# Spectral mixing, then a leaky-ReLU MLP: the exchange of real and imaginary products in the second batch, by DMA for every group instead of every other one

## The chip, the cores and the metric

The kernel runs on one core of a Trainium2 chip. The core has a matrix engine (TensorE, "PE" in the profile, with "PEld" for the loading of weights), a vector engine (VectorE, "DVE"), a scalar engine (ScalarE, "ACT"), GpSimd ("POOL") and SyncE ("SP"), which here only issues DMAs. The metric is the device time of one execution in microseconds, lower is better.

## What is computed

The reference, cut to what matters:

```python
X = np.fft.rfft(x, axis=1)                     # x: 8 x 3008 x 256, fp32
Y = X * (filt_r + 1j * filt_i)[None, :, :]
y = np.fft.irfft(Y, n=3008, axis=1)
h = y.reshape(24064, 256) @ w_in               # 256 x 2048
g = np.maximum(0.01 * h, h)
out = g @ w_out                                # 2048 x 256
```

## The kernel before

The Fourier transforms are matrix products: 3008 is 94 x 32, so each transform is a product with a 94-point matrix, a change of layout, and a product with 32-point matrices that also hold the twiddle factors. All matrix operands are fp16, sums are fp32 in PSUM.

The eight batches b = 0 to 7 follow each other. Each batch goes through four stages, each cut into groups:

- `s1_group` (lines 249 to 261, 16 groups): one matmul on the rows of x (L254), a copy to SBUF, and a store to the DRAM buffer `dz1` (L259). `t1_load` (L266) reads it back in the new layout, as `z1`.
- `s2_group` (lines 297 to 319, 12 groups): two matmuls (L303) give 128 x 512 fp32 in a PSUM bank. Partitions 0 to 63 hold real parts, 64 to 127 imaginary parts. The complex product with the filter needs `ps * fa` (p1, L315) plus the same bank times `fb` with the two halves of partitions exchanged (p3). GpSimd adds the two as `y` (L318).
- `sa_group` (12 groups): one matmul on `y` (L325), a copy by ACT (L327), a store to `dz2` (L329). `t2_load` (L273) reads it back as `z2`.
- `sb_group` (16 groups): four matmuls (L346) and a copy give `yt`, the input of the MLP.

The exchange of halves in `s2_group` is made in two ways. As a rule VectorE writes `p2 = ps * fb` (L312), and two DMAs on SP's queue copy its halves crosswise into p3 (L313, L314). In the second batch (b = 1), where g is even (`EXG = 0`), VectorE writes p3 itself with two products on 64 partitions each (L309, L310), which read one half of the bank and write the other half of p3.

p1, p2 and p3 are tiles of 128 x 512 fp32 from the pool `scr`, which has three buffers for each of the three tags. Six more tiles with the same tags (`spare`) serve the first batch, two of each tag.

The first batch (b = 0) is written out step by step in a table and takes about 34 us. After that the MLP runs in chunks of 512 tokens: `moe1` makes h (L505) with ACT applying the leaky ReLU (L510), and `plain` (L630, the first chunks) or `products` (L569, a fast scheme with seven products) make the output. The groups of the transforms of later batches are put between the MLP's matmuls.

The order of all this is a plan worked out at build time: each piece of work gets a time in units of an eighth of a chunk, and `work`, a heap, hands the pieces out in order of time. `at` and `soon` put pieces on it; `soon(AFTER[1], ...)` puts the two exchange DMAs 0.8 units after the product, and `y_delay` says how long after the group the add on GpSimd stands: 1.2 units where VectorE exchanges, 3.17 (`AFTER[3]`) for the other groups of b = 1, 1.33 (`AFTER[2]`) for later batches. Once made, the order on each engine is fixed; each engine, and each queue of DMAs (SP's, GpSimd's), works through its own list in order and waits where a tile is not ready. GpSimd's list also has the loads of x for the next batch (L191).

The small groups (L254, L303, L325, L346, and the last groups of the first batch, L437) take turns on two PSUM banks, called `pf` in the profile like a third one that holds the output of the MLP. Finished outputs are copied to SBUF by VectorE (L635 in the first chunks) and stored by SP (L556).

Of the kernel before, what the change touches and what calls it, by code (L numbers as in the profile page):

```python
# [11 lines left out]
P = 128  # L12
FP16 = mybir.dt.float16
FP32 = mybir.dt.float32
AL = mybir.AluOpType
# [60 lines left out]
def kernel(  # L76
# [9 lines left out]
    nc = tc.nc  # L86
    B, N, D = x.shape
# [8 lines left out]
    SL = 8  # L96
    NCH = NCT // 2
    QT = 4 * N1
    W0 = 3
    GAP = 0.6  # L100
    EXG = 0
    LANDED = 2.43
    READ = 2.2
    SUMS = (0.09, 1.59, 2.35, 4)
# [5 lines left out]
    AFTER = (0.53, 0.8, 1.33, 3.17, 0.39, 0.52)  # L110
# [31 lines left out]
    scrp = ctx.enter_context(tc.tile_pool(name="scr", bufs=3))  # L142
# [11 lines left out]
    def bank(kind, n, w):  # L154
        of = wide if kind == "ph" else single
        t = of[turn[kind] % len(of)]
        turn[kind] += 1
        return t[:, : n * w].rearrange("p (n w) -> p n w", n=n)
# [5 lines left out]
    def at(time, f):  # L164
        clock["n"] += 1
        heapq.heappush(work, (time, clock["n"], f))
# [4 lines left out]
    def need(*what):  # L171
        for w in what:
            assert w in issued, w

    def noted(what, f):
        f()
        issued.add(what)

    def soon(delay, f):
        at(clock["now"] + delay, f)  # L180
# [5 lines left out]
    DH = D // 2  # L186
# [105 lines left out]
    ys = {}  # L292

    def y_delay(b, g):
        return 1.2 if b == 1 and g % 2 == EXG else AFTER[2] if b > 1 else AFTER[3]

    def s2_group(b, g):
        def go():
            ps = bank("pf", 2, D)
            need(("z1", b, g // 2), ("f2t",))  # L300
            issued.add(("s2", b, g))
            for j in range(2):
                nc.tensor.matmul(ps[:, j, :], f2_sb[:, 2 * g + j, :],  # L303
                                 z1[g // 2 % 4][:, 2 * (g % 2) + j, :],
                                 start=True, stop=True)
            fa, fb = fa_sb[:, ds(2 * g, 2), :], fb_sb[:, ds(2 * g, 2), :]
            p1, p2, p3 = (scrp.tile([P, 2, D], FP32, tag=f"p{i}", name=f"p{i}_b{b}_g{g}") for i in (1, 2, 3))
            if b == 1 and g % 2 == EXG:
                nc.vector.tensor_tensor(p3[0:64], ps[64:P], fb[64:P], AL.mult)  # L309
                nc.vector.tensor_tensor(p3[64:P], ps[0:64], fb[0:64], AL.mult)  # L310
            else:
                nc.vector.tensor_tensor(p2[:], ps, fb, AL.mult)  # L312
                soon(AFTER[1], lambda: nc.sync.dma_start(p3[0:64], p2[64:P]))  # L313
                soon(AFTER[1], lambda: nc.sync.dma_start(p3[64:P], p2[0:64]))  # L314
            nc.vector.tensor_tensor(p1[:], ps, fa, AL.mult)  # L315
            ys[(b, g)] = y1 = ypp.tile([P, 2, D], FP16, tag="y", name=f"y_b{b}_g{g}")
            soon(y_delay(b, g), lambda: noted(
                ("y", b, g), lambda: nc.gpsimd.tensor_tensor(y1[:], p1[:], p3[:], AL.add)))  # L318
        return go
# [13 lines left out]
    def quad_copy(h, dt, ps, copy):  # L333

        yv = yt[:, dt, ts(h, QT)].rearrange("p (a c) -> p a c", c=4)
        copy(yv, ps.rearrange("p c a -> p a c"))  # L336

    def sb_group(b, g, copy):
        h, dt = g // 2, g % 2

        def go():
            ps = bank("pf", 4, N1)
            need(("z2", b, h), ("i1t",))
            issued.add(("sb", b, g))
            for j in range(4):
                nc.tensor.matmul(ps[:, j, :], z2[h % 4][:K4, j, ts(dt, P)], i1_sb[:K4, 4 * h + j, :],  # L346
                                 start=True, stop=True)
            quad_copy(h, dt, ps, copy)
        return go
# [6 lines left out]
    prods = [gtp.tile([P, 2, NC, DH], FP16, tag="gt", padded_shape=[P, 2, Q, DH], name=f"prod{hf}")  # L356
             for hf in range(2)]
    first_banks = single + wide
    held, spare = {}, [scrp.tile([P, 4, DH], FP32, tag=f"p{i // 2 + 1}", name=f"spare{i}") for i in range(6)]
    engine = {"A": act, "D": dve}  # L360

    def fill(key, b, n, w):
# [185 lines left out]
    def store(ci, tj, of, queue=nc.sync):  # L548
# [3 lines left out]
        while t < end:  # L552
            e = min(end, (t // QT + 1) * QT)
            b, h = divmod(t // QT, N2 // 4)
            row = b * N + (t % QT) // 4 * N2 + 4 * h
            queue.dma_start(  # L556
# [35 lines left out]
    def last_product(ci):  # L592
        def after(po):
            add(rows(ci, 0)[:, :, 1], po, rows(ci, 1)[:, :, 2], AL.add)
            soon(AFTER[5], lambda: stores(ci, 0))
        return product(ci, lambda: sum_places(ci)[3], b22, after, 3)

    def products(ci):
        a11, a12, a21, a22 = (lambda i=i, j=j: quarter(ci, i, j) for i in range(2) for j in range(2))

        def after5(po):
            add(rows(ci, 1)[:, :, 1:3], twice(po), part[1], AL.add)
            soon(AFTER[5], lambda: stores(ci, 1))

        def m1():
            return product(ci, a11, b11, lambda po: nc.scalar.copy(t1, po))

        def m2():
            return product(ci, a12, b21, lambda po: add(rows(ci, 0)[:, :, 0], po, t1, AL.add))

        def m7():
            return product(ci, lambda: sum_places(ci)[1], wt[2], lambda po: add(v7, po, t1, AL.add), 1)

        if ci == NCHUNK - 1:
            items = last_product(ci - 1) + m1() + m7() + m2()
        elif ci > W0:
            items = m1() + last_product(ci - 1) + m2() + m7()
        else:
            done["products"] += 1
            items = m1() + [lambda: None] * (2 * NCH) + m2() + m7()  # L620
        items += product(ci, lambda: sum_places(ci)[2], wt[1], lambda po: add(part[1], twice(po), part[0], AL.add), 2)
        items += product(ci, a22, wt[3], lambda po: add(rows(ci, 1)[:, :, 0], po, u3, AL.add))
        items += product(ci, lambda: sum_places(ci)[0], wt[0], after5, 0)
        return items + last_product(ci) if ci == NCHUNK - 1 else items

    def plain(ci):

        def one(tj, ct):
            po = out_banks[(done["products"] + tj) % 2].rearrange("p a t d -> p (a t d)")[:, :D]
            nc.tensor.matmul(po, gts[ci][:, ct, ts(tj, P)], w_out_sb[:, ct, :],  # L630
                             start=(ct == 0), stop=(ct == NCT - 1))
            if ct < NCT - 1:
                return
            ot = outp.tile([P, D], FP32, tag="ost", padded_shape=[P, 6 * P], name=f"ost_c{ci}_t{tj}")
            nc.vector.tensor_copy(ot[:], po)  # L635
            soon(AFTER[5], lambda: store(ci, tj, ot[:]))
        return [lambda tj=tj, ct=ct: one(tj, ct) for tj in range(4) for ct in range(NCT)]
# [5 lines left out]
    def plan(b, s1, s1_step, s2, s2_step, lag, sb, sb_step, xl, x_step):  # L643
# [9 lines left out]
        for g in range(16):  # L653
            due = SL * (QT * (8 * b + g // 2) // CH)
            groups.append((min(sb + sb_step * g, due - DUE[0] + DUE[1] * (g % 2)), 4, b, g, sb_group(b, g, act)))
# [13 lines left out]
    for b in range(1, B):  # L669
        z = 47 * (b - 4) if b > 4 else 0  # L670
        p = PLANS[min(b, 4) - 1]
# [18 lines left out]
    while queue:  # L690
        time, n, stage, b, g, f = heapq.heappop(queue)
        t = max(time, last + GAP)
        if stage == 3:
            behind = when[2, b, g] + y_delay(b, g) + 0.02 if (2, b, g) in when else None
        else:
            behind = load_time(stage - 1, b, g // 2) if stage != 1 else 0
            if stage != 1 and behind is not None:
                behind += READ
        if behind is None or behind + 0.02 > t:
            heapq.heappush(queue, (t + GAP if behind is None else behind + 0.03, n, stage, b, g, f))  # L700
            continue
        when[stage, b, g] = last = t
        at(t, f)
        if stage in (2, 4) and g % 2:
            place[stage - 1, g // 2 % 4] = t + 0.1
        assert stage < 4 or t < SL * (QT * (8 * b + g // 2) // CH), (b, g, t)

    for ci in range(NCHUNK + 1):
# [3 lines left out]
        if ci == 0:  # L712
            continue
        wino = W0 <= ci - 1
        items = products(ci - 1) if wino else plain(ci - 1)
# [38 lines left out]
```

## Time and profile before

| | |
|---|---|
| median of 3 runs | 749.61 us (749.38 to 750.32) |
| the profiled execution | 749.61 us |
| its span, first to last instruction | 747.8 us |
| granted TensorE clock | 0.999 |
| DMA traffic | 113.64 MB, mean 152 GB/s |
| first batch, before the MLP starts | about 34 us |
| second batch's `s2` groups | 59.9 to 91.5 us |
| second batch's `sa` groups | 70.1 to 100.8 us |
| third batch's `s2` groups begin | 118.3 us |

The profile is of one execution. A page sums it up: busy time of each engine, the chain of work that ended last, the costliest groups of instructions. Views of its trace show the engines by stretches of time, what each engine waited for, and the instructions in order of time. In a timeline a line has the start in us, the length in us, the engine ("SPq" is the issue of a DMA by SP), the line of the kernel, the operation, what it writes and reads, and in brackets how long the engine was idle before it and what ended that.

### The profile page before, as it was taken

The page shows a single profiled execution, that of the slowest core. Times are in us where ns is not written, and L with a number is a line of the kernel's source. Part 1 is how long each engine was busy: PE and PEld are TensorE (multiplying, and loading weights), DVE is VectorE, ACT ScalarE, POOL GpSimd, SP SyncE. Part 2 cuts the span into 40 slices and gives each one's busy share as a digit, 9 for nine tenths or more (in the row PEclk, how much of TensorE's full clock was granted, in tenths as well). Part 3 has the DMA queues.
Part 4 walks back from the last instruction along what each step waited for, and adds up shares of the span by engine and source line. Part 5 has one row for each costly group of instructions (what it writes and reads, how often), then busy time and mean ns, then how long its engine had stood idle before and what let it go on. Part 6 is the DMA issues. An engine that isn't in the chain of part 4 may idle for free.

```text
span 747.8 us, 19408 instructions
## 1 busy us (share of the span) xinstructions
PE 737.9 (99%) x8017; PEld 528.6 (71%) x8017; DVE 499.9 (67%) x684; ACT 559.1 (75%) x755; POOL 167.5 (22%) x171
## 2 busy tenths in 40 slices
PE   8999999999999999999999999999999999999996
PEld 3556667776787777877778777777777777777775
DVE  6977647766686666776767667766676675565565
ACT  4776797888878787877777778787777777777662
POOL 6503422332323213221222322121212220000000
PEclk9999999999999999999999999999999999999999
DMA  9997798887876666755675656544454333111111
GB/s 207 228 222 190 187 226 222 210 193 202 208 189 149 161 183 175 169 142 161 195 173 150 158 165 170 157 131 111 143 168 119 97 108 104 50 56 53 34 52 59
DMA packets 119560, 113.64 MB, mean 152 GB/s; under 512 B 16352, under 2 KB 92768, under 8 KB 119280
## 3 DMA queue, kind: packets, MB, share of 16 engines
q1 hardware_dynamic: 104127, 94.66, 43.0%
q0 software_dynamic: 15056, 17.49, 15.9%
q8 instruction: 62, 1.02, 0.6%
q10 hardware_dynamic: 289, 0.26, 0.1%
q14 instruction: 26, 0.21, 0.1%
HBM read 57.51 MB, written 50.33 MB: 144 GB/s over the span
## 4 chain that ended last, share of the span: by engine, by line
PE 93%; DMA 2%; DVE 2%; ACT 1%; issue 0%; POOL 0%; SPq 0%; DVEq 0%; POOLq 0%
PE ph L505 42%; PE po_ps L569 18%; PE pf L569 18%; PE pf L254 3%; PE pf L346 3%; PE pf L303 2%; PE pf L325 2%; DMA p_b_g<-p_b_g 2%; PE pf L630 1%; PE po_ps L630 1%; DMA big<-in_x_dram 1%; PE po_ps L368 1%; POOL y_b_g L318 0%; ACT yt L336 0%; PE ph L396 0%
## 5 line engine op out<-in xcount | busy, mean ns | idle before, releaser
L510 ACT ACTIVATE gt_c<-ph 128x1024 f16<-128x1024 f32 x376 | 385.3, 1025 | 135.2 <-PE ph L505 123.5
L505 PE MATMUL ph<-yt,w_in_sb 128*128 128x512 f16 (+7 forms) x1728 | 447.5, 351 | 0.2 <-ACT yt L336 0.2
L569 PEld LDWEIGHTS <-gt_c 128*128 128x128 f16 x2800 | 202.1, 98 | 91.3 <-issue 0.2
L318 POOL TENSOR_TENSOR y_b_g<-p_b_g,p_b_g 128x512 f16<-128x512 f32 x84 | 117.8, 1403 | 415.0 <-DMA p_b_g<-p_b_g 255.2
L569 PEld LDWEIGHTS <-big 128*128 128x128 f16 x2128 | 151.2, 98 | 61.6 <-issue 0.2
L505 PEld LDWEIGHTS <-w_in_sb 128*128 128x128 f16 x1728 | 137.4, 98 | 20.3 <-issue 0.7
L312 DVE TENSOR_TENSOR p_b_g<-pf,fb_sb 128x512 f32<-128x512 f32 x78 | 53.7, 688 | 32.3 <-PE pf L303 17.2
L569 PE MATMUL po_ps<-wt_sb,gt_c 128*128 128x128 f16 x704 | 70.0, 219 | 0.0
L569 PE MATMUL pf<-wt_sb,gt_c 128*128 128x128 f16 x688 | 68.5, 219 | 0.0
L569 PE MATMUL pf<-w_out_sb,gt_c 128*128 128x128 f16 x720 | 68.0, 219 | 0.0
L569 PE MATMUL po_ps<-wt_sb,big 128*128 128x128 f16 x720 | 67.5, 219 | 0.0
L569 PE MATMUL pf<-wt_sb,big 128*128 128x128 f16 x704 | 67.2, 219 | 0.0
L257 ACT CAST big<-pf 128x512 f16<-128x512 f32 x100 | 58.3, 588 | 11.9 <-PE pf L254 10.5
L569 PE MATMUL po_ps<-w_out_sb,gt_c 128*128 128x128 f16 x688 | 66.0, 219 | 0.0
L336 ACT CAST yt<-pf 128x376 f16<-128x376 f32 x120 | 56.3, 473 | 10.7 <-PE pf L346 7.7
L315 DVE TENSOR_TENSOR p_b_g<-pf,fa_sb 128x512 f32<-128x512 f32 x84 | 57.2, 681 | 0.2
L542 DVE TENSOR_TENSOR big<-gt_c 128x2048 f16<-128x2048 f16 (+1 forms) x46 | 57.0, 1238 | 0.1
L542 DVE TENSOR_TENSOR big<-gt_c,big 128x2048 f16<-128x2048 f16 (+1 forms) x45 | 55.3, 1228 | 0.0
L542 DVE TENSOR_TENSOR gt_c<-gt_c 128x2048 f16<-128x2048 f16 x43 | 54.6, 1269 | 1.0
L542 DVE TENSOR_TENSOR big<-big,gt_c 128x2048 f16<-128x2048 f16 (+1 forms) x45 | 54.6, 1212 | 0.1
L327 ACT CAST big<-pf 128x512 f16<-128x512 f32 x84 | 49.0, 584 | 4.9 <-PE pf L325 3.0
L254 PE MATMUL pf<-x_sb,small_sb 94*128 94x512 f16 x112 | 42.7, 381 | 0.6 <-ACT big L257 0.6
(88 smaller groups left out, 620.3 us busy)
## 6 DMA issues: line engine op xcount, KB each, us to landing
dz<-big SPq DMA_DIRECT2D x98, 256.0 KB
p_b_g<-p_b_g SPq DMA_DIRECT2D x156, 128.0 KB
out_dram<-ost_c_h SPq DMA_DIRECT2D x119, 128.0 KB
big<-dz SPq DMA_DIRECT2D x42, 256.0 KB
big<-dz SPq DMA_DIRECT2D x56, 192.0 KB
x_sb<-in_x_dram POOLq DMA_DIRECT2D x40, 192.0 KB, 4.7
x_sb<-in_x_dram POOLq DMA_DIRECT2D x2, 768.0 KB, 9.6
w_in_sb<-in_moe_w_in_dram POOLq DMA_DIRECT2D x1, 1024.0 KB, 13.7
```

The lines of the kernel that those rows point to most:

```text
L254: nc.tensor.matmul(ps, fwd1[:N1], x_sb[:N1, ds(2 * g, 2), :], start=True, stop=True)
L257: copy(st[:, ds(2 * (g % 2), 2), :], ps)
L312: nc.vector.tensor_tensor(p2[:], ps, fb, AL.mult)
L315: nc.vector.tensor_tensor(p1[:], ps, fa, AL.mult)
L318: ("y", b, g), lambda: nc.gpsimd.tensor_tensor(y1[:], p1[:], p3[:], AL.add)))
L327: nc.scalar.copy(st2[h % 4][:, ds(2 * (g % 2), 2), :], ps)
L336: copy(yv, ps.rearrange("p c a -> p a c"))
L346: nc.tensor.matmul(ps[:, j, :], z2[h % 4][:K4, j, ts(dt, P)], i1_sb[:K4, 4 * h + j, :], start=True, stop=True)
L505: nc.tensor.matmul(ph[:, j, ds(t - ci * CH, e - t)], w_in_sb[:, dt, ts(ct, P)], yt[:, dt, ds(t % N, e - t)], start=(dt == 0), stop=(dt == ...
L510: nc.scalar.activation(gts[ci][:, ds(2 * g, 2), :], ph, AF.Lrelu)
L542: nc.vector.tensor_tensor(*(v[:, ds(c0, n)] for v in (o, i0, i1)), op)
L569: nc.tensor.matmul(po[:, t], a()[:, c, ts(t, P)], w[:, c, :], start=(c == 0), stop=(c == NCH - 1))
```

## The change

In the second batch every group now takes the way by DMA. The two half products, `EXG` and the shorter delay of their add go. The pool's three buffers for each of p1, p2 and p3 become four for p1, two for p2 and four for p3, for `spare` too.

```diff
+    SCR = (4, 2, 4)
...
-    EXG = 0
...
     def y_delay(b, g):
-        return 1.2 if b == 1 and g % 2 == EXG else AFTER[2] if b > 1 else AFTER[3]
+        return AFTER[2] if b > 1 else AFTER[3]
...
-            p1, p2, p3 = (scrp.tile([P, 2, D], FP32, tag=f"p{i}", name=f"p{i}_b{b}_g{g}") for i in (1, 2, 3))
-            if b == 1 and g % 2 == EXG:
-                nc.vector.tensor_tensor(p3[0:64], ps[64:P], fb[64:P], AL.mult)
-                nc.vector.tensor_tensor(p3[64:P], ps[0:64], fb[0:64], AL.mult)
-            else:
-                nc.vector.tensor_tensor(p2[:], ps, fb, AL.mult)
-                soon(AFTER[1], lambda: nc.sync.dma_start(p3[0:64], p2[64:P]))
-                soon(AFTER[1], lambda: nc.sync.dma_start(p3[64:P], p2[0:64]))
+            p1, p2, p3 = (scrp.tile([P, 2, D], FP32, tag=f"p{i}", bufs=SCR[i - 1], name=f"p{i}_b{b}_g{g}")
+                          for i in (1, 2, 3))
+            nc.vector.tensor_tensor(p2[:], ps, fb, AL.mult)
+            soon(AFTER[1], lambda: nc.sync.dma_start(p3[0:64], p2[64:P]))
+            soon(AFTER[1], lambda: nc.sync.dma_start(p3[64:P], p2[0:64]))
             nc.vector.tensor_tensor(p1[:], ps, fa, AL.mult)
```

In the order of instructions on each engine this moves little. PE and ACT have the same instructions in the same order. VectorE has six fewer. SP has twelve DMAs more, those of groups 0, 2, 4, 6, 8 and 10. On GpSimd the adds of the second batch now stand in the order of the groups (before, the add of an even group stood ahead of that of the odd group before it), and the third load of x stands ahead of the first add instead of behind it.

More of the change, by code (lines that the diff above doesn't have):

```diff
@@ L358 @@
     first_banks = single + wide
-    held, spare = {}, [scrp.tile([P, 4, DH], FP32, tag=f"p{i // 2 + 1}", name=f"spare{i}") for i in range(6)]
+    held, spare = {}, [scrp.tile([P, 4, DH], FP32, tag=f"p{i // 2 + 1}", bufs=SCR[i // 2], name=f"spare{i}") for i in range(6)]
     engine = {"A": act, "D": dve}
```

## The prediction

> **What bounds the kernel now.** I read the page first, then the stretches, the waits of PE, and the timelines of DVE, SP and POOL between 55 and 112 us, where the changed groups stand. Page, part 1 (busy us, share of the span, instructions):
>
> ```profile
> PE 737.9 (99%) x8017; PEld 528.6 (71%) x8017; DVE 499.9 (67%) x684; ACT 559.1 (75%) x755; POOL 167.5 (22%) x171
> ```
>
> PE is busy nearly always; what counts is time in which PE stands still. Stretches of 5 us (length, PE, PEld, DVE, ACT, POOL busy, clock, DMA share, GB/s) and PE's waits from 55 to 100 us (total, times, longest):
>
> ```profile
> 60.00:65.00 5.00, 5.00 (x37) 3.42 (x36) 4.69 (x9) 2.12 (x4) 1.76 (x2) 1.00 0.69 213
> 65.00:70.00 5.00, 4.09 (x30) 2.64 (x28) 4.44 (x8) 2.59 (x4) 2.53 (x2) 1.00 0.88 194
> 70.00:75.00 5.00, 5.00 (x41) 3.22 (x40) 2.50 (x5) 4.10 (x6) 3.02 (x3) 1.00 0.56 123
> ```
>
> ```profile
> PE pf L303 <- DVE p_b_g L315: 0.9, 1, 0.9
> ```
>
> In the whole stage PE stands still once, 0.91 us before 66.14, when group 3 of the second batch (b=1) wants the PSUM bank that group 2's last product (L315) still reads; the next gap of over 0.05 us is 0.07 us at 196.6. So the change can gain at most about 1 us, and each new wait of PE here moves the end by its full length. The bank rule matters below: two `pf` banks in turn serve all small groups, so the second user after a group waits for that group's L315. DVE in this stage:
>
> ```profile
> 60.34 0.69 DVE L309 TENSOR_TENSOR p_b_g<-pf,fb_sb 64x512 f32<-64x512 f32 x1 [0.24 <-PE pf L303]
> 61.05 0.68 DVE L310 TENSOR_TENSOR p_b_g<-pf,fb_sb 64x512 f32<-64x512 f32 x1
> 61.75 0.69 DVE L315 TENSOR_TENSOR p_b_g<-pf,fa_sb 128x512 f32<-128x512 f32 x1
> 62.35 0.68 DVE L312 TENSOR_TENSOR p_b_g<-pf,fb_sb 128x512 f32<-128x512 f32 x1
> 62.95 0.68 DVE L315 TENSOR_TENSOR p_b_g<-pf,fa_sb 128x512 f32<-128x512 f32 x1
> 63.55 0.42 DVE L635 COPY ost_c_t<-pf 128x256 f32<-128x256 f32 x1
> 64.00 0.69 DVE L309 TENSOR_TENSOR p_b_g<-pf,fb_sb 64x512 f32<-64x512 f32 x1
> ...
> 91.52 0.69 DVE L312 TENSOR_TENSOR p_b_g<-pf,fb_sb 128x512 f32<-128x512 f32 x1 [0.28 <-PE pf L303]
> ```
>
> An operation on 64 partitions costs as much as one on 128. From the start of p2 to the end of p1 a group takes 1.28 us (62.35 to 63.63). SP's queue, which issues the exchanges (L313, L314), and one POOL add:
>
> ```profile
> 61.46 0.33 SPq L266 DMA_DIRECT2D big<-dz  x1
> 63.11 0.56 SPq L313 DMA_DIRECT2D p_b_g<-p_b_g  x1
> 63.72 0.59 SPq L314 DMA_DIRECT2D p_b_g<-p_b_g  x1
> ...
> 86.87 1.77 SPq L556 DMA_DIRECT2D out_dram<-ost_c_t  x2
> 88.76 0.53 SPq L313 DMA_DIRECT2D p_b_g<-p_b_g  x1
> 89.34 0.60 SPq L314 DMA_DIRECT2D p_b_g<-p_b_g  x1
> ```
>
> ```profile
> 68.27 1.27 POOL L318 TENSOR_TENSOR y_b_g<-p_b_g,p_b_g 128x512 f16<-128x512 f32 x1 [0.82 <-DMA p_b_g<-p_b_g]
> ```
>
> When SP's DMAs landed I counted from the landing semaphores in the trace: L314 of 63.72 at 68.13 (the add starts 0.14 later), of 67.99 at 70.86, of 75.75 at 78.17, of 80.37 at 84.66, of 89.34 at 92.54, of 92.80 at 95.20. So a second half lands 2.4 us after its issue when nothing is in the way, and up to 4.4.
>
> **The change, part by part.** *Removed:* 12 half products in groups 0, 2, 4, 6, 8, 10 (6 x 0.69 + 6 x 0.68 = 8.2 us of DVE). *Added:* 6 full ones (4.1 us) and 12 DMAs of 128 KB (6 x 0.53 + 6 x 0.59 = 6.7 us of SP issue, 1.5 MB between 61 and 95 us). DVE's saving of 4.1 us is worth nothing by itself: DVE waited for PE ahead of most groups from group 5 on (0.28 to 1.96 us each); only group 2's share touches PE's one gap.
>
> *The new wait.* p2 has two buffers instead of three, and now every group uses one: group g's p2 must wait until the exchange of group g-2 has landed (before, only odd groups used p2, so a buffer came back after six groups). Behind the waiting product on DVE stand its own p1, the copy of a finished output and the next group; for p1 waits the PSUM bank, and for that PE. I go through the groups on the time axis of before.
>
> A, group 2. SP issues the load of 61.46, then group 0's halves at about 61.9 and 62.45 (p2 ready at 61.03). The load lands at 64.74. The same pattern at 66.56: load landed 70.55, halves 70.70 and 70.86, 0.3 behind the load. So group 0 lands at about 65.25; plus 0.14, 1.28 and 0.04 (L315's end to PE's start), group 3 starts at 66.71 instead of 66.14: **+0.6**. Bounds: landing 2.4 after issue gives 64.85 and +0.2; 4.4 gives 66.85 and +2.2.
>
> Here a page of the Trainium skill has a price: "DMA: Bandwidth & Descriptors", section "Anatomy of one DMA", fits 2.0 us plus bytes over 436 GB/s for GpSimd's queue, an estimate of 2.3 us for 128 KB. By it group 0 would land at 64.75 and A would be 0.1; the quiet rows agree with it, the rows behind a load do not, and the load decides here.
>
> B, group 4. From group 2's p2 start: 0.68 product, 0.08 to SP, 0.61 to the second half's issue, 2.42 landing, 0.14, then 1.28: 5.21 us. The next user of that bank (L325, 70.06) is due 1.28 + 0.04 + 3.92 = 5.24 after the same point. Nothing is left over; +0.03 slack against a spread of landings up to 3.2 (67.47): 0 to 0.8, taken **+0.1**, near the quiet row, as the x load that stood at 63.74 moves away.
>
> C, group 11. Its p2 ran at 91.52, but group 9's exchange, which SP issues only at 88.76 behind two stores, lands at 92.54. 92.54 + 0.14 + 1.28 + 0.04 = 94.0, and the bank's next user (L325) stood at 93.39: **+0.6**. Bounds: landing 2.4 after issue (91.74) gives nothing, 4.4 gives +1.8; the row of this very exchange lies between.
>
> Groups 5, 7, 9: the exchange of g-2 landed 0.9, 0.3 and 0.6 us ahead of the old p2 start (70.86 and 71.74, 78.17 and 78.44, 84.66 and 85.22), and their banks have another 0.5 us. Group 3: exchange 1 keeps its issue (63.1) and loses the x load beside it. Groups 6, 8, 10 start 5.6 us or more after the product of g-2, against 3.1 us from product to landing. All nothing, if the landings hold.
>
> E, the turn to the second transform. The last store of `dz2` is issued at 101.86, lands at 107.16 in a crowded queue (5.3 us), the loads follow at 107.18 and land from 109.65, and PE uses the first at 110.09: 0.4 us to spare. Exchange 10 adds 256 KB and exchange 11 comes about 1.2 us later, as do the x loads behind POOL's last add; four 256 KB loads landed 0.6 to 0.7 apart (59.72 to 61.65). So 0 to +0.9, taken **+0.3**.
>
> *Moved at no cost:* POOL's six adds wait for exchanges now; the adds are wanted by L325 at 70.06, 72.44, 76.83, 80.79 and later, and the landings above leave over 1.5 us. The third x load goes from 63.74 to about 39, among transfers that had all landed by 53.1, 2.5 us before the loads (55.62) that need them; this frees the time in which exchange 1 was slow. The i1 matrix is issued 1.1 us later (83.28) and first used at 110. Orders on PE and ACT do not change. In the batches from the third on, two p2 buffers suffice: the tightest exchange landed at 159.09, the next but one p2 began at 161.67, 2.6 us later. Four buffers for p1 and p3 gain nothing: no product waited for an add.
>
> A second page speaks against counting stalls in full: "Perfetto Trace Analysis", section "Identifying the Most-Contended Engine", calls matmul busy time a bad measure and asks for weight loads, here 71%. By it PE had room and the sum could shrink to 0. The chain of waits shows two 512-column matmuls in 0.43 us with no gap behind 66.5; I take the row.
>
> **Sum.** 0.6 + 0.1 + 0.6 + 0.3 = 1.6 us. The profiled execution spans 747.8 and took 749.61 (1.8 outside), which is also the median of the runs: 747.8 + 1.6 + 1.8 = **751.2 us**. 0.2%, about what a measurement of this kernel can tell from no change, is 1.5 us, so the forecast lies just over that bound.
>
> **Rivals.**
> 1. *Forecast, slower by little* (0.43): the waits as summed, 751.1 to 752.3.
> 2. *The wait is mostly hidden* (0.36), not slower: exchanges land 2.4 us after issue, C and E vanish, A is 0.2 to 0.6: 749.8 to 750.2, up to 751.1 if one of the two stays. For it: the earlier x load clears the queue. Against: 64.74 and 92.54. It decides if exchange 9 lands before 91.9.
> 3. *The wait feeds itself* (0.15): landings of 4.4 us instead of 2.4 at groups 2, 4 and 11, 2.2 + 0.8 + 1.8 less overlap, about +3.5: 753. Each exchange starts from the product that waited for the one before, so a late one delays the next. It decides once exchange 0 lands after 66.
> 4. *Lighter DVE wins* (0.06): exchange 0 lands by 63.8, the 0.91 us gap goes: 748.7. Against: its issue is at 62.45. A gain over 0.2% has no gap to come from; I leave 0.04 for what I have not seen.
>
> Chances: slower 0.43 + 0.15 = 0.58, same 0.36 + 0.02 = 0.38, faster 0.04. The range takes rival 2's lower part, the forecast and most of rival 3: 749.5 to 753.0.
>
> **What would show it.** Right: PE's waits in this stage name L315's successor at about 66.7 (total 1.5 us) and an L325 near 94; DVE's p2 of groups 2 and 11 waits for DMA p_b_g; nothing changes behind 112. Wrong: no DVE wait for an exchange (rival 2), waits at groups 4, 7 or 9 too (rival 3), the gap at 66 gone (rival 4), or new waits in later batches.

## The result, and the profile after

| | before | after |
|---|---|---|
| median | 749.97 us (4 runs, 749.38 to 751.10) | 753.15 us (4 runs, 752.63 to 753.98) |
| ratio | | 1.0042, 95% interval 1.0024 to 1.0059 |
| the profiled execution, its span | 749.61, 747.8 us | 753.98, 752.2 us |

The changed kernel is slower by 3.2 us, twice the 1.6 us forecast, and 0.15 us above the predicted range. Its code is three lines shorter there, so the products p2 and p1 are now L309 and L312, the two exchange DMAs L310 and L311, the add L315, and the first matmuls of the second transform L343.

What answers to the first two views of before is part 1 of the page and PE's waits between 55 and 130 us (total, times, longest):

```profile
PE 739.0 (98%) x8017; PEld 529.7 (70%) x8017; DVE 498.2 (66%) x678; ACT 559.6 (74%) x755; POOL 167.9 (22%) x171
```

```profile
PE pf L343 <- DMA big<-dz: 2.4, 1, 2.4
PE pf L303 <- DVE p_b_g L312: 1.6, 1, 1.6
```

The gap near 66 has grown from 0.91 to 1.60 us, as term A said. The large one is new: near 111 PE waits 2.39 us for the first load of `z2`. Term E gave this turn 0.3. The stretches around it, cut where the clock changes (length, PE, PEld, DVE, ACT, POOL busy, granted clock, DMA share, GB/s), show a third thing:

```profile
106.70:110.15 3.45, 3.45 (x37) 2.37 (x36) 1.12 (x2) 3.30 (x5) 0.00 (x0) 1.00 0.75 219
110.15:113.56 3.41, 1.02 (x14) 0.57 (x11) 0.00 (x0) 1.10 (x2) 0.00 (x0) 1.00 0.63 187
113.56:116.97 3.41, 3.41 (x26) 2.29 (x23) 0.42 (x1) 0.94 (x2) 0.00 (x0) 0.50 0.76 224
116.97:120.40 3.43, 3.43 (x46) 2.58 (x45) 2.92 (x3) 2.66 (x4) 0.00 (x0) 1.00 0.78 222
```

Behind the gap TensorE ran at half its clock for 3.41 us; PE shows as busy there, with 26 matmuls where the next stretch of that length has 46.

I also laid the starts of PE's 8017 matmuls side by side, which is possible because their order is the same. After minus before is under 0.2 in size from 10 to 60 us and -0.10 just ahead of the gap near 66, 0.59 behind it, 3.17 behind the gap near 111, 4.82 behind the half clock, 4.56 at the end. So in this pair of executions 0.7 is the first gap, 2.6 the second, 1.65 the clock, and little (0.26 the other way) changes in the 635 us that follow. The profiled execution of the changed kernel is the slowest of its four; what the clock has to do with that is taken up below.

Where the second gap comes from is in three timelines of the changed kernel. First the last p2 of the batch on DVE, then SP with the second half of exchange 9 (89.95) and the last exchange, then GpSimd:

```profile
92.66 0.69 DVE L309 TENSOR_TENSOR p_b_g<-pf,fb_sb 128x512 f32<-128x512 f32 x1 [1.69 <-DMA p_b_g<-p_b_g]
```

```profile
89.95 0.62 SPq L311 DMA_DIRECT2D p_b_g<-p_b_g  x1
...
93.41 0.48 SPq L310 DMA_DIRECT2D p_b_g<-p_b_g  x1
93.94 0.59 SPq L311 DMA_DIRECT2D p_b_g<-p_b_g  x1
...
102.47 0.37 SPq L326 DMA_DIRECT2D dz<-big  x1
105.28 0.36 SPq L259 DMA_DIRECT2D dz<-big  x1
110.23 1.74 SPq L273 DMA_DIRECT2D big<-dz  x4
```

```profile
93.91 1.03 POOL L191 DMA_DIRECT2D x_sb<-in_x_dram  x2
94.95 1.28 POOL L315 TENSOR_TENSOR y_b_g<-p_b_g,p_b_g 128x512 f16<-128x512 f32 x1
98.55 1.27 POOL L315 TENSOR_TENSOR y_b_g<-p_b_g,p_b_g 128x512 f16<-128x512 f32 x1 [2.32 <-PE pf L322]
99.75 1.52 POOL L191 DMA_DIRECT2D x_sb<-in_x_dram  x3
```

And the same place before, the second half of the last exchange, the last store of `dz2` and the `z2` loads on SP, then GpSimd:

```profile
92.80 0.59 SPq L314 DMA_DIRECT2D p_b_g<-p_b_g  x1
...
101.86 0.36 SPq L329 DMA_DIRECT2D dz<-big  x1
...
107.18 1.74 SPq L273 DMA_DIRECT2D big<-dz  x4
```

```profile
93.91 1.03 POOL L191 DMA_DIRECT2D x_sb<-in_x_dram  x2
95.33 1.27 POOL L318 TENSOR_TENSOR y_b_g<-p_b_g,p_b_g 128x512 f16<-128x512 f32 x1 [0.39 <-DMA p_b_g<-p_b_g]
96.54 1.53 POOL L191 DMA_DIRECT2D x_sb<-in_x_dram  x3
```

Group 11's p2 waits for exchange 9, so its own exchange is issued 1.1 us later (93.94 instead of 92.80 for the second half). That is 0.03 behind an x load that GpSimd issues at 93.91, where before it was 1.1 ahead of it. By the landing semaphores the half needed 4.44 us instead of 2.41, and landed at 98.39 instead of 95.20. The add at 98.55 waits for that (the view names PE's L322, the last releaser that it saw, but L322 had long run), and the three x loads queued behind the add go out at 99.75 instead of 96.54. The last store of `dz2`, issued only 0.6 later than before (102.47), now shares its way with them: it lands at 110.18 after 7.7 us instead of at 107.16 after 5.3. SP issues the `z2` loads at 110.23, and PE gets the first at 113.26.

That the half meets the x load is no accident of this execution. The landing of exchange 9 (92.53) releases both: the add of group 9, behind which the x load goes out 1.38 us after the landing, and group 11's p2, whose second half goes out 1.41 us after it. In the four runs below that also have two p2 buffers and exchange groups 9 to 11 by DMA, the half was issued 0.02 to 0.14 us behind an x load, and needed 4.43 to 4.57 us.

So **my theory** was now: A costs 0.7; a delay of 1.1 us at group 11's p2 is turned into 3.2 by an x load and into 2.4 on PE; and the half clock is a consequence of the second gap. **The rivals**: the extra DMA traffic itself costs the time, whatever the buffers; the late loads have another cause; the half clock is a matter of its own.

### The profile page after: what moved, and what is told of

It reads as the page before. It is cut to its first block, busy times and chain, and to the rows that moved or that the text cites. A ratio compares the mean times of both kernels' runs of the same rounds, so it can differ in the third digit from the quotient of the medians.

```text
span 752.2 us, 19419 instructions
## 1 busy us (share of the span) xinstructions
PE 739.0 (98%) x8017; PEld 529.7 (70%) x8017; DVE 498.2 (66%) x678; ACT 559.6 (74%) x755; POOL 167.9 (22%) x171
## 4 chain that ended last, share of the span: by engine, by line
PE 92%; DMA 4%; DVE 1%; ACT 1%; issue 0%; POOL 0%; SPq 0%; DVEq 0%; POOLq 0%
PE ph L502 42%; PE po_ps L566 18%; PE pf L566 18%; PE pf L254 3%; PE pf L343 3%; PE pf L303 2%; PE pf L322 2%; DMA dz<-big 2%; DMA x_sb<-in_x_dram 1%; PE po_ps L627 1%; PE pf L627 1%; PE po_ps L365 0%; DMA big<-dz 0%; ACT yt L333 0%; DMA p_b_g<-p_b_g 0%
## 5 line engine op out<-in xcount | busy, mean ns | idle before, releaser
L315 POOL TENSOR_TENSOR y_b_g<-p_b_g,p_b_g 128x512 f16<-128x512 f32 x84 | 118.2, 1408 | 416.4 <-DMA p_b_g<-p_b_g 248.6
L309 DVE TENSOR_TENSOR p_b_g<-pf,fb_sb 128x512 f32<-128x512 f32 x84 | 57.8, 688 | 42.6 <-PE pf L303 21.3
L312 DVE TENSOR_TENSOR p_b_g<-pf,fa_sb 128x512 f32<-128x512 f32 x84 | 57.2, 680 | 0.0
```

## The experiments

Each ratio is to the kernel before, run on the same chip, with its 95% interval. An edit that adds or takes lines shifts the line numbers in its profile; the operations and tiles tell what is what.

### Which part of the change costs the time

Three buffers for each tag, as before; the exchange by DMA stays:

```diff
-    SCR = (4, 2, 4)
+    SCR = (3, 3, 3)
```

> The changed kernel with three buffers again for each of p1, p2 and p3; all exchanges by DMA as in the change. Theory 1 (p2's two buffers make both new stalls of PE: at group 2 directly, at the first product of the inverse's second half because group 11's product, its exchange, the last add and so the x loads behind it come late and crowd the last dz2 stores): group 2's product no longer waits for an exchange, the PE gap near 66 us goes or stays under 0.3 us, the gap near 111 us is under 0.5 us, time 748.6 to 749.6 us. Theory 2 (the 1.5 MB of added exchanges crowd the queues, whatever the buffers): the gap near 66 goes, that near 111 stays at 1.5 to 2.5 us, time 751 to 752.5 us.

Measured: 750.21 us, ratio 1.0004 (0.9995 to 1.0013). PE's waits:

```profile
PE pf L343 <- DMA big<-dz: 0.5, 1, 0.5
PE pf L254 <- DVE p_b_g L312: 0.3, 1, 0.3
```

With the same twelve extra DMAs the loss is gone, so traffic alone is not what costs it. The gap near 66 has gone altogether. Yet the time is not below that of the kernel before, as was expected (748.6 to 749.6): 0.3 came back at the next group, where p1 waited for one of its three buffers, and 0.5 near 111.

The buffers alone, in the kernel before (the halves stay on VectorE):

```diff
-    (no SCR; bufs=3 for p1, p2 and p3)
+    SCR = (4, 2, 4)
...
+    ... bufs=SCR[i - 1] ... bufs=SCR[i // 2]
```

> The kernel before with the buffers of the change (four, two, four) and its own way of exchanging: even groups of the second batch on VectorE. Theory 1: only odd groups use p2, so two buffers suffice; 749.3 to 750.3 us, one PE gap of 0.9 us near 66 and none near 111. Rival (two buffers hurt by themselves, in later batches too): 751 us or more.

Measured: 749.95 us, ratio 0.9995 (0.9986 to 1.0004), the gap near 66 at 0.95 as before, none near 111. Two p2 buffers cost nothing while only every other group uses one. It takes both halves of the change.

Then the DMA exchange for half of the groups each. For 6, 8 and 10 (VectorE keeps 0, 2 and 4):

```diff
+    EXG = (0, 2, 4)
...
-            (p2 and two DMAs for every group)
+            if b == 1 and g in EXG:
+                (two half products, and the short delay of the add)
```

> Buffers as in the change (four, two, four); groups 0, 2 and 4 of the second batch exchanged on VectorE as before, groups 6, 8 and 10 by DMA. Both theories: the gap near 66 us is 0.9 us as before. Theory 1: group 11's product still waits for exchange 9, so the gap near 111 stays at 1.5 to 2.6 us, time 751.3 to 753 us. Theory 2 (bytes): half of the bytes, a gap near 111 of 0.5 to 1.5 us, 750.3 to 751.5 us.

and for 0, 2 and 4 (`EXG = (6, 8, 10)`):

> Buffers as in the change; groups 0, 2 and 4 by DMA, groups 6, 8 and 10 on VectorE. Theory 1: the gap near 66 is 1.5 to 1.7 us, no product of group 11 waits for an exchange, no gap near 111: 750.2 to 750.8 us. Theory 2: a gap near 111 of 0.5 to 1.5 us as well, 751 to 752 us.

Measured: 752.35 us, 1.0032 (1.0020 to 1.0044), and 751.18 us, 1.0018 (1.0008 to 1.0027). PE's waits of the first, then of the second:

```profile
PE pf L347 <- DMA big<-dz: 1.6, 1, 1.6
PE pf L304 <- DVE p_b_g L316: 0.9, 1, 0.9
```

```profile
PE pf L304 <- DVE p_b_g L316: 1.6, 1, 1.6
```

By these profiles the change falls apart into two losses that come separately: the early groups make the gap near 66 and nothing near 111, the late ones leave the gap near 66 as it was and make the one near 111. The time of the second run is not explained so well. Its profiled execution (749.96) is the fastest of eleven, and the median is 1.4 us above the kernel before, where this profile shows 0.7; it lies in the range of theory 2 (751 to 752), above that of theory 1 (750.2 to 750.8). The missing gap near 111 speaks for theory 1; what made the other executions slower shows in part in their clocks, below. With the late groups, p2 waited 2.0 us for exchange 9, exchange 11 landed at 98.95, and the x loads went out at 100.32; with the early ones these loads went out at 96.84.

### Are the late x loads the link?

The changed kernel with the last three x loads ahead of the last two adds on GpSimd's queue:

```diff
-                at(s1 + xl + x_step * g, lambda g=g: (need(("s1", b, g)), noted(
+                due = s1 + xl + x_step * g
+                at(29.9 if b < 3 and 29.9 < due < 39 else due, lambda g=g: (need(("s1", b, g)), noted(
```

> The changed kernel, but in GpSimd's list the three loads of x that stand behind the last two adds of the second batch stand ahead of them. Theory 1 as it stands now (the gap near 111 us comes from these loads: the last add waits for exchange 11, so they are issued at 99.75 instead of 96.5 and lie in front of the last dz2 stores): issue near 95, last dz2 store lands by 107.8, gap near 111 under 0.6 us, the gap of 1.6 near 66 stays, 750.2 to 751.0 us. Rival (the exchanges themselves fill the queue there): gap near 111 stays over 1.5 us, 752 us or more.

Measured: 751.56 us, ratio 1.0015 (1.0007 to 1.0024). The only wait of PE left in this stretch:

```profile
PE pf L303 <- DVE p_b_g L312: 1.8, 1, 1.8
```

The loads are out by 97.8, the last `dz2` store takes 4.9 us, though it is issued later than in the changed kernel (104.06, landed 108.94), and the gap near 111 is gone with its half clock. What is left is the gap of term A, 1.75 here. The time is above the expected 750.2 to 751.0, but beside this run the kernel before had 750.45, 0.5 above its 749.97 beside the changed kernel.

The reverse, in the kernel before: three adds on an extra tile (`spin`) on GpSimd hold the same three loads up, and nothing else is touched:

```diff
+            if (b, g) == (1, 11):
+                for i in range(3):
+                    soon(y_delay(b, g), lambda: nc.gpsimd.tensor_tensor(spin[:], idle[:], idle[:], AL.add))
```

> The kernel before, with three adds on a scratch tile on GpSimd behind the last add of the second batch (about 3.8 us together), which hold back the three loads of x that follow; nothing else is changed. Theory 1: late loads alone suffice: the last dz2 store lands near 110, a PE gap of 1.5 to 2.7 us near 110, 751.3 to 753.5 us. Rival (bytes or stores of the change are needed too): gap under 0.5 us, 749.5 to 750.2 us.

Measured: 752.18 us, ratio 1.0025 (1.0014 to 1.0036). GpSimd, then PE's waits:

```profile
96.97 4.13 POOL L322 TENSOR_TENSOR spin<-idle 128x512 f16<-128x512 f16 x3
101.05 1.52 POOL L191 DMA_DIRECT2D x_sb<-in_x_dram  x3
```

```profile
PE pf L350 <- DMA big<-dz: 1.6, 1, 1.6
PE pf L304 <- DVE p_b_g L316: 1.0, 1, 1.0
```

The last store was issued at 102.27, 0.4 later than in before, and took 7.2 us. Late loads are enough to make the gap; the exchanges and the buffers are not needed for it.

### Is it the load ahead of exchange 0?

Term A blamed the `z1` load that SP issues just ahead of exchange 0. In the changed kernel the load goes behind the exchanges:

```diff
-                                         when[end] + AFTER[4 * (stage // 2)] + LANDED)
+                                         when[end] + AFTER[4 * (stage // 2)] + LANDED) + 1.5 * ((stage, b, c) == (1, 1, 4))
```

> The changed kernel, but on SP's queue the load of z1 that stood ahead of exchange 0 (61.36 us) is issued some groups later. If the load in front and the wait for it on SP set the landing of exchange 0: it is issued near 61.0 and 61.6, lands near 64.0 instead of 65.3, and the PE gap near 66 falls from 1.6 to 0.2 to 0.5 us; with the gap near 111 unchanged the time is 1.1 to 1.4 us under the changed kernel's. If the landing is set by the issue on SP and the time in flight alone, 0.7 us of the gap go.

Measured: 753.51 us, ratio 1.0038 (1.0025 to 1.0051). PE's waits and DVE's sum of waits for exchanges:

```profile
PE pf L343 <- DMA big<-dz: 2.1, 1, 2.1
PE pf L303 <- DVE p_b_g L312: 0.9, 1, 0.9
PE pf L322 <- DVE p_b_g L312: 0.8, 1, 0.8
```

```profile
DVE p_b_g L309 <- DMA p_b_g<-p_b_g: 8.2, 5, 2.6
```

SP's exchange 0 in the changed kernel, then in this run:

```profile
61.75 0.82 SPq L310 DMA_DIRECT2D p_b_g<-p_b_g  x1
62.61 0.59 SPq L311 DMA_DIRECT2D p_b_g<-p_b_g  x1
```

```profile
61.34 0.55 SPq L310 DMA_DIRECT2D p_b_g<-p_b_g  x1
61.95 1.14 SPq L311 DMA_DIRECT2D p_b_g<-p_b_g  x1
```

The gap near 66 is back to 0.89: exchange 0 landed at 64.87 instead of 65.27, although its product ended 0.3 later in this execution (61.25 instead of 60.93), and that is the 0.7 by which the gap shrank. So the load ahead of the exchange was the cause of A, but by its place on SP: the second half was issued 0.70 us behind the product's end instead of 1.68, and needed no less time from issue to landing (2.93 us, against 2.66 with the load ahead). That is the second case of the expectation; the landing near 64.0 did not come.

The time did not fall by 1.1 to 1.4 us as expected, because a gap of 0.82 near 94 has taken the place of A, ahead of the L322 that wants the bank of group 11. That is term C, which the changed kernel did not show. In the changed kernel PE came to this matmul at 94.00, just when the bank was free. Here PE was 0.40 earlier (group 3 at 66.34 instead of 66.74). The second half of exchange 9 was issued earlier by as much (89.56 instead of 89.95), but needed 3.53 us instead of 2.58 and landed later, at 93.10 instead of 92.53. So it is the longer landing that brought C out, not the absence of A; what made it longer is not shown.

### The half clock

The changed kernel with twelve matmuls on a tile of zeros (128 x 376, result not used) in the gap near 111:

```diff
+            if (b, g) == (1, 0):
+                for i in range(12):
+                    nc.tensor.matmul(ps, idle[:, 0:P], idle[:, : 4 * N1].rearrange("p (n w) -> p n w", n=4),
+                                     start=True, stop=True)
```

> The changed kernel with twelve matmuls on zeros (128 x 376, about 0.16 us each, 1.9 us together) just ahead of the group that waits near 111 us; their result is overwritten. If PE's standing still for 2.4 us is what halves the clock for the 3.4 us behind it: no time at half clock in the profile, 751.4 to 752.4 us, no worse than the changed kernel. If the half clock has another cause: it appears in the same place, and the time is that of the changed kernel, 752.6 to 754.

Measured: 754.26 us, ratio 1.0048 (1.0036 to 1.0060): no gain. The filler kept PE busy for 2.07 us, and neither gap nor half clock is seen there. But in this execution the gap near 66 was 2.23 us long, and the half clock came behind that one:

```profile
66.00:68.70 2.70, 0.47 (x4) 0.38 (x4) 1.34 (x3) 0.18 (x1) 1.77 (x2) 1.00 0.33 96
68.70:72.20 3.50, 3.50 (x16) 1.99 (x14) 2.80 (x5) 1.02 (x1) 2.25 (x3) 0.51 0.80 220
```

By its own question the run settles nothing on the time. Near 111 the gap without the filler would have been some 1.2 us by this trace (the matmul ahead of it ended at 114.02, the first `z2` load landed at 115.20). But the half clock stands behind a gap in another place here, and is missing where PE was busy. Over the kernels so far, gaps of 2.07 (the load behind the exchanges), 2.23 and 2.39 us were followed by 3.41 us of half clock, and gaps of 1.60 to 1.75 us were not. So I measured gaps by themselves. This kernel computes nothing of the reference:

```python
for k, j in enumerate(order):                    # 42 gaps, 14 lengths
    for i in range(BURST + k % 7):               # BURST = 70
        nc.tensor.matmul(ps[k % 2][:], w[:], m[:], start=True, stop=True)
    wide = 40 + 280 * j
    nc.vector.tensor_copy(s[0][:, 0:1], ps[k % 2][:, 0:1])
    nc.vector.tensor_copy(s[1][:, 0:wide // 2], s[0][:, 0:wide // 2])
    nc.vector.tensor_copy(s[0][:, 0:wide // 2], s[1][:, 0:wide // 2])
    nc.vector.tensor_copy(w[:, 0:1], s[0][:, 0:1])
```

> The cost of a gap in TensorE's work by itself: this kernel computes nothing of the reference. It runs 42 bursts of 70 to 76 matmuls of 128 x 512 (15 to 16 us each) with gaps between them that a chain of four VectorE copies sets, 14 lengths from some 1 us to some 3 us or more, each three times. Theory 1 (a gap of 2 us or more brings the half clock, a gap of 1.75 or less does not; the length alone decides): every gap over 2.07 us is followed by 3.4 us at a granted clock of 0.5, none under 1.75 is. Theory 2 (where the gap falls against some interval of 3.4 us decides): lengths between about 1.7 and 3.4 us are followed by it in some of the three cases and not in others. Theory 3 (the half clock of the changed kernel has nothing to do with the gap): it comes after none of them, or without regard to length.

Measured, in one execution: 41 gaps between bursts, of 0.86 to 2.81 us. No gap of 1.88 or less was followed by the half clock. Of the 18 of 2.02 or more 13 were, and 5 were not (2.17, 2.31, 2.31, 2.46, 2.75). So length alone does not decide, and theory 2 holds. The records tell what does: every half clock starts at a multiple of 3.4133 us from every other, to 0.01 us (112.05, 166.66, 204.21, 224.69 ...; the last two are 6 x 3.4133 apart). Between these marks I counted how long PE stood still:

| longest standstill between two marks | gaps | followed by half clock |
|---|---|---|
| 0.65 to 1.91 us | 27 | 0 |
| 2.02 to 2.06 us | 5 | 4 |
| 2.13 to 2.81 us | 9 | 9 |

A gap of 2.02 us between two marks (at 201.22), and one of 2.75 us (at 694.50) that a mark cuts into 1.2 and 1.5, in stretches (length, PE, PEld, DVE, POOL busy, clock, DMA share, GB/s):

```profile
200.80:204.20 3.40, 1.38 (x7) 0.49 (x6) 1.82 (x4) 0.00 (x0) 1.00 0.00 0
204.20:207.60 3.40, 3.40 (x10) 1.23 (x9) 0.00 (x0) 0.00 (x0) 0.50 0.01 2
692.30:695.70 3.40, 2.20 (x11) 0.78 (x8) 1.12 (x2) 0.00 (x0) 1.00 0.00 0
695.70:699.10 3.40, 1.85 (x9) 0.90 (x10) 1.43 (x3) 0.00 (x0) 1.00 0.02 5
699.10:702.50 3.40, 3.40 (x18) 1.53 (x16) 0.00 (x0) 0.00 (x0) 1.00 0.00 0
```

The changed kernel fits: its 2.39 us (110.87 to 113.26) lie wholly in the 3.41 us ahead of 113.56, where its half clock began. The marks do not follow the kernel: counted back in steps of 3.4133 us, the first one lies at 0.9 us in the profile of the changed kernel (from 113.56) and at 1.9 in that of the kernel before (from 746.00, where the half clock of its last microseconds began). So an execution meets them by chance. A gap of 2.39 us has 2.0 of its length between two marks for 1.80 of the 3.41 us over which its start can fall (from 0.39 ahead of a mark to 1.41 behind it), 53 in 100. By this estimate the clock costs the changed kernel 1.65 us in about half of its executions.

The mean granted clock of every execution is on record and bears on this. A half clock of 3.41 us takes 0.0023 from the mean; the last microseconds, which are at half clock in all profiles of the kernels, take up to that again. So a mean of 0.999 or 1.000 leaves no room for one, 0.998 leaves it open, and the two profiles with less than 0.998 both show one. The four executions of the changed kernel have 0.998 (753.98, the profiled one), 0.998 (752.98), 0.999 (753.33) and 1.000 (752.63). At least two of them had none, 753.33 among them, which is 3.4 above the median of before: the loss does not need the clock, and the clock alone does not make the spread of the four. In the runs for groups 0, 2 and 4, for the loads ahead, for the load behind the exchanges, for the filler and for the late loads in the kernel before, eight executions have less than 0.998, and they are the slowest of their kernels.

The Trainium skill, "TensorE: Matmul & The Clock Gate", Part 1 on the clock gate, has the same free-running window of 3413 ns. Its rule under "HAM oscillation", that a standstill must not exceed some 3.4 us, is too mild by these runs: some 2.0 us inside one window were enough.

### A version that keeps the exchange and loses the waits

Three buffers for p2, four for p1 and p3; and the same with the x loads ahead of the last two adds, as above:

```diff
-    SCR = (4, 2, 4)
+    SCR = (4, 3, 4)
```

> The changed kernel with three buffers for p2 and four for p1 and p3 (4, 3, 4). With (3, 3, 3) PE still stood 0.29 us behind a p1 that waited for its buffer, and 0.53 near 111. Theory 1 (the two p2 buffers cost the time; the DMAs themselves are free): no PE gap between 60 and 100 us, so 0.9 below the kernel before in that stage; a gap of 0 to 0.55 near 111; together 0.4 to 0.9 us below the kernel before, 749.0 to 749.5 by a median of 749.9. Theory 2 (the exchanges by DMA cost PE time by their traffic, whatever the buffers): a gap near 66 of 0.3 or more, and a time no better than before.

> As the last, and the three x loads stand ahead of the last two adds on GpSimd's queue. Theory 1 (the late x loads are what holds up the last store of dz2): the x loads are issued at 95 to 97 us, the last dz2 store lands by 108, no gap near 111, and the time is 0 to 0.5 us below the last kernel's, 0.9 below the kernel before. Theory 2 (near 111 the 256 KB exchanges of groups 10 and 11 count, not the loads): a gap of 0.4 or more near 111 and the time of the last kernel.

Measured: 749.80 us, ratio 0.9991 (0.9981 to 1.0000), and 748.72 us, ratio 0.9972 (0.9964 to 0.9981). PE's waits of the second, from 55 to 260 us:

```profile
PE pf L343 <- DMA big<-dz: 0.3, 1, 0.3
PE pf L343 <- DVE p_b_g L312: 0.2, 1, 0.2
```

The gap near 66 is gone in both. Near 110 the first has 0.92 in its profile, more than the 0 to 0.55 expected, the second 0.26: theory 1 again. The second beats both kernels. Yet its gain is larger than expected: 0.5 by the gaps in the profiles, 0.9 if the turn cost nothing, and 2.1 measured. In part the profiles understate it: that of the kernel before is of a fast execution (749.61; the 22 executions beside this run have 749.64 to 753.02). One more run asked where the rest came from, the kernel before with only the loads moved ahead (the edit shown above):

> The kernel before, with the three x loads ahead of the last two adds on GpSimd's queue, and nothing else. It tells where the last kernel's gain of 2.1 us came from, of which its profile shows 0.3 to 0.9. Theory 1 (in many executions of the kernel before, the last dz2 store is late enough for a gap near 111 that its one profile, with 0.4 us to spare, does not show): 0.5 to 1.3 us below the kernel before, and the rest of the 2.1 is the gap near 66. Theory 2 (the turn to the second transform costs the kernel before nothing): within 0.3 us of it; the PE gap near 66 stays at 0.9 in both cases.

Measured: 749.95 us, ratio 0.9996 (0.9987 to 1.0005). That is 0.3 below the kernel before, as theory 2 had it: alone, the moved loads gain little or nothing. The interval reaches to 1.0 below, so the lower part of theory 1 (0.5 to 1.3) is not excluded. Its profiled execution (751.08, the slowest of eleven) had one gap that no other profile has, 1.13 us at 211 (L325 waits for an add of the fourth batch):

```profile
PE pf L325 <- POOL y_b_g L318: 1.1, 1, 1.1
PE pf L303 <- DVE p_b_g L315: 0.9, 1, 0.9
```

Single gaps of this kind may be what some executions of before have and the last version lacks; with one profile for each kernel that is a guess. About 1 us of the last version's gain, or somewhat more, stays open.

## Why the prediction was wrong

Its direction and its main cause were right: two p2 buffers used by every group make p2 wait for exchanges, and PE pays. The failure is in the size, and it lies in one term above all.

- **E, the turn to the second transform, is the step that failed**: +0.3, with 0 to 0.9 as bounds, where the trace has 2.4 to 2.6 and another 1.65 of half clock in that execution. The step said that "exchange 11 comes about 1.2 us later, as do the x loads behind POOL's last add". The first half held (1.1). The second did not: exchange 11's second half slipped behind an x load of the other queue, and add and loads came 3.2 later. With these loads moved ahead the gap was gone, and with them held up in the kernel before it was there (1.6). I had laid exchange 11 against SP's own list only. The x load at 93.91 stood in GpSimd's timeline, and a delay of 1.1 put 93.94 right behind it; the row of 63.72, landed after 4.41 with an x load issued 0.02 us behind it, had shown the price, and I used it as an upper bound for A and C, not here. The upper bound of 0.9, from four loads landing 0.6 to 0.7 apart, was no bound: with three late x loads the last store took 7.7 us instead of 5.3. The slack was smaller than stated, too: the last part of the first `z2` load landed at 109.84, not 109.65, 0.25 ahead of its use.
- **The clock** was in no term. The profile of before gave no cause to fear it, having no gap over 0.91 behind the first batch. A gap of 2.39 that I priced at 0.3 could not raise the question.
- **A, +0.6**: 0.69 in PE's gap; exchange 0 landed at 65.27, forecast 65.25. The cause, the `z1` load ahead of it on SP, was shown by putting it behind, but the close agreement is partly luck. The step let the exchange land 0.3 behind the load of 64.74; that is 65.05 and +0.4, not the 65.25 that it wrote. The load landed at 64.43 and the second half 0.84 behind it, and what counted was the half's late issue on SP. Other profiles with the same exchanges near 66 have gaps of 1.62, 1.75 and 2.23 there, 0.7 to 1.3 over the 0.91, and where A alone is left the medians rose by 1.1 and 1.4.
- **B, +0.1**: no PE gap. p2 of group 4 waited 0.71 at 69.15, which the bank's slack held.
- **C, +0.6**: 0. The wait on DVE came (p2 waited 1.69 for exchange 9), the one on PE did not. PE was 0.60 late by A, and exchange 9 with it: its second half was issued at 89.95 instead of 89.34. But it needed 2.58 us where the row of before has 3.20, and so landed at 92.53, as before; the bank was free just as PE came to it. With 3.20, by the same sum, the term would have cost its 0.6. With 3.53 it cost 0.82, and where groups 0, 2 and 4 stayed on VectorE, so that A was absent, 2.38 us left 0.15. The term hung on one landing time, which differed from execution to execution; that it came out at 0 was chance as far as is known.
- **At no cost**: VectorE's saved 4.1 us was worth nothing, as said, and the adds' order and the four buffers for p1 and p3 did no harm. In the batches from the third on the exchange of g-2 landed at least 2.4 us ahead of each p2 (the view names an exchange for two waits of DVE, at 162.04 and 218.82, but the one needed had long landed), PE had no gap over 0.05 us up to 740, and its lag went from 4.82 at 117 us to 4.56 at the end.
- **The page against counting stalls in full**, the Trainium skill's "Perfetto Trace Analysis", section "Identifying the Most-Contended Engine": it speaks of how close a kernel is to its roofline, and that PE had room for a stall was the prediction's reading of it. In this trace the two gaps and the half clock (0.69, 2.56 and 1.65) make up the lag of 4.56 at the end but for 0.3.
- **Rivals**: 753 was the price of the wait that feeds itself, and the time came out there, but not by that road. Exchange 0 landed at 65.27, ahead of its turning point of 66, and of the groups named as signs only 4 waited, without cost to PE. The third rival's number was right for a wrong reason.

## What to carry to other kernels

Where an instruction is delayed, go through what the *other* queues issue in the stretch into which it moves: 1.1 us at one product put a DMA behind another queue's load, and that made it 3.2 us at an add and 2.4 us on TensorE. Look as well for what one landing releases on two queues: the two DMAs that the landing of exchange 9 set free met in all five profiles. A wait that hangs on one landing time needs the range of the landings seen: for the same exchange 2.4 to 3.5 us made term C anything from 0 to 0.8. And price a standstill of TensorE of 2 us or more higher than its length, by another 1.65 us in some executions.

## What the runs showed of the hardware

- The granted clock fell to 0.5 for 3.41 us where TensorE had stood still for some 2.0 us or more between two marks that lie 3.4133 us apart (13 of 14 cases from 2.02 us up, none of 27 up to 1.91 us). The half clock began at the second mark.
- A copy of 128 KB within SBUF took 2.4 us when issued 1.1 us ahead of an x load of another queue, and 4.4 to 4.6 us in five profiles when issued 0.02 to 0.14 behind one. The same 4.4 us was in the trace of before, where an x load was issued 0.02 us behind it.
- Three x loads issued 3.2 us later, 2.7 to 1.7 us ahead of a store of 256 KB instead of 5.3 to 4.3, went with 7.7 us for that store instead of 5.3. Held up alone, in the kernel before, they went with 7.2 us; moved ahead, in the changed kernel, with 4.9.
